# Q and K of a banded attention kernel cut into full 128-row tiles, with the static order retuned

A kernel for sliding-window attention followed by a mixture of adapters was already tuned. One change regroups the rows of queries and keys so that every transpose works on a full tile, retunes the order in which the engines' work is emitted, adds matmuls at the start that only keep TensorE busy, and moves the fetching of the adapter weights.

## The chip, the cores and the metric

The kernel runs on one core of one Trainium2 chip. The metric is device time in microseconds of one execution. Each run is marked fast or slow (slow: over 1.5% above the fastest run of the same kernel), and comparisons use fast runs. A ratio below is the mean time of one kernel's fast runs over that of the other's of the same rounds, so it is not quite the ratio of the medians that I quote. Its 95% interval is in brackets. A profile shows one execution, and its span is about 1.7 us shorter than the time of that run.

Engines in the profile: PE is TensorE (matmuls), PEld its weight loads, DVE is VectorE, ACT ScalarE, POOL GpSimd, SP SyncE, whose queue (SPq) issues nearly all transfers (36.58 of 38.27 MB in before).

## The reference

Eight batches of eight heads, 576 positions, 64 channels. Attention sees a band of 32 positions to each side. The 512 attention outputs of a position are then the input of a two-of-eight mixture of rank-16 adapters.

```python
scores = (q @ k.transpose(0, 1, 3, 2)) / np.sqrt(64)       # [8, 8, 576, 576]
scores = np.where(np.abs(pos[:, None] - pos[None, :]) <= 32, scores, -1e9)
attn = softmax(scores)
x = (attn @ v).transpose(0, 2, 1, 3).reshape(8 * 576, 512)
logits = x @ w_gate                                         # [4608, 8]
# the two largest logits of a row, softmax over the two: weights w
delta = sum over the two chosen e of  w[e] * (x @ A[e]) @ B[e]   # ranks 16
out = x + delta
```

q, k, v are normal with deviation 0.1, so the scores are tiny and the softmax inside the band is nearly flat.

## The kernel before

A batch is worked on as four units; a unit is a pair of heads (n and n + 4), whose 64 channels each fill 128 partitions once transposed. The steps, with the names that the profile uses:

1. load q, k, v from memory as float32 into `r` tiles (SyncE's queue, in order);
2. POOL casts them to float16: `c` for q and k, `vbd` for v;
3. PE transposes q and k into the PSUM tile `tp`; DVE and ACT copy it to `qT` and `kT`;
4. PE forms score tiles `ps` (first the mask, then q against k), ACT takes the exponential into `PT`;
5. PE multiplies with v into `po`, DVE normalizes into `xb`;
6. adapters: PE transposes (`tx`), multiplies with gate and A (`pz`), DVE computes the gate and the gated product `zs`, PE transposes it (`tz`) and multiplies with B (`pd`), ACT copies out (`obt`), SyncE's queue stores.

With 576 positions split into pairs of neighbours, one head has 288 rows of 128 values: two full tiles of 128 rows and a stub of 32.

```python
    def load_qk(b, w, eng, n0=0, n1=NP):
        ...
        src = (q, k)[w][b].rearrange("(e n) (p j) d -> e p n (j d)", e=2, j=2)
        for g in range(3):                       # two full row groups and the stub
            r0, r1 = 128 * g, min(128 * g + 128, S // 2)
            if g < 2:
                dst = raw[b, w][:, g]
            else:
                dst = raw[b, 3][32 * w:32 * w + 32]
            ...
    def transposes(u, which, holder):            # one unit, q or k
        ...
        for g in range(3):
            p0, np_ = (0, 128) if g < 2 else (32 * which, 32)
            for j in range(2):
                ...
                nc.tensor.matmul(
                    out=o, lhsT=src[:, g, j, n] if g < 2 else sx[p0:p0 + 32, j, n],
                    rhs=ident[p0:p0 + np_, p0:p0 + np_], is_transpose=True,
                    start=True, stop=True)
```

So a unit takes four full transposes and two stubs for q and as many for k: eight groups of six a batch, 48 in all, 16 of them stubs.

The weights of the adapters are fetched on POOL's queue right at the start, in pieces that transfer and convert at once (0.27 MB in 4832 packets):

```python
    def load_weights():
        for c in range(4):
            nc.gpsimd.dma_start(out=WA_sb[:, c, 0:ER],
                in_=moe_A.transpose([1, 0, 2])[128 * c:128 * c + 128])
        nc.gpsimd.dma_start(out=WA_sb[:, :, ER:],
            in_=moe_w_gate.rearrange("(c p) e -> p c e", p=128))
        nc.gpsimd.dma_start(out=B_sb, in_=moe_B.rearrange("e r d -> (e r) d"))
```

The order of the instructions on each engine is static. A small scheduler inside the program lists all operations with estimated durations and a due time each, simulates, and emits them in the order found. The due times come from one table, in units of a quarter batch (`DUE`: `ld` loads, `cqk` casts of q and k, `cv` cast of v, `tq` and `tk` transposes, `g0` and `g3` the gate, and so on). When an operation has to wait, what stands behind it on the engine waits too: in g, below, six casts of q and k stand behind a V cast with which POOL waits 6.0 us, and start right after the V casts.

The softmax here doesn't subtract the row's maximum and nothing guards it: scores larger than these inputs give would overflow.

## Time and profile before

| | before |
|---|---|
| median, 3 runs | 175.34 us (174.99 to 175.36) |
| span of the profiled execution | 172.3 us |
| PE busy | 137.2 us |
| first transpose starts | 11.4 us |
| pace, gate of batch 1 to gate of batch 6, by batch | 16.9 us |

From the page of before: part 1 (busy time, share of span, instructions) and three rows of part 2, in which each character is one fortieth of the span, 4.3 us, and a digit is tenths of busy time (PE), of granted TensorE clock (PEclk) or of the 16 DMA engines' time (DMA).

```profile
PE 137.2 (80%) x1600; PEld 103.4 (60%) x1600; DVE 113.8 (66%) x290; ACT 85.0 (49%) x109; POOL 85.0 (49%) x91
...
PE   0028596699957999999599989997999899969180
...
PEclk9999999659995699999999999999999999999968
DMA  5999999999999899999999997976889603403425
```

Three stretches show. PE is idle at first, uneven until slice 14 (60 us) with two dips of the clock (0.50 at 32 to 38 us, 0.52 at 52 to 58), then nearly full until slice 35 (150 us). DMA is full from the second slice to the 24th. Both PE and DMA are candidates for the limit in the middle.

The idle start, in the table of waits of before (waiting engine and line, what ended the wait: total us, times, longest) and in the timeline of POOL (start, duration, engine, line, operation):

```profile
PE tp L360 <- POOL c L197: 11.6, 2, 11.4
```

```profile
5.73 3.74 POOL L263 DMA_DIRECT2D WA_sb<-in_moe_A_dram  x4
...
10.74 1.20 POOL L197 CAST c<-r 128x512 f16<-128x512 f32 x2
```

The first transpose waited 11.4 us for a cast on POOL, which was issuing weight transfers until 10.7.

The transposes in the groups of before, different shapes apart (line, engine, operation, output and input, shape, count, busy us and mean ns of one, idle time before them and what ended it):

```profile
L360 PE MATMUL tp<-ident,c 128*128 128x128 f16 x256 | 28.0, 238 | 21.4 <-POOL c L197 11.6 <-DVE qT L366 8.1 <-ACT kT L376 1.6
L360 PE MATMUL tp<-ident,c 32*128 32x32 f16 x128 | 13.7, 181 | 2.4 <-POOL c L204 2.4
...
L360 PEld LDWEIGHTS <-c 128*128 128x128 f16 x256 | 19.1, 104 | 23.9 <-POOL c L197 12.8 <-issue 9.2
L360 PEld LDWEIGHTS <-c 32*128 32x128 f16 x128 | 7.2, 95 | 10.6 <-POOL c L204 3.1 <-issue 2.4
```

The records of the stubs, 181 ns, are little shorter than those of full tiles, 238 ns. The records overlap: a group's four and two come to 1.3 us at these means, and below the group takes 0.46. The timeline of PE in before, in the full stretch:

```profile
85.31 0.61 PE L409 MATMUL ps<-qT,kT 128*128 128x128 f16 x8
85.76 0.53 PE L360 MATMUL tp<-ident,c 128*128 128x128 f16 x6
86.22 0.60 PE L404 MATMUL ps<-mask,ident 128*128 128x512 f16 x2
```

A group of six (four full and two stubs) starts at 85.76 and the next work at 86.22: 0.46 us.

### The profile page before, as it was taken

How to read it: one execution, taken by the hardware profiler on the slowest of the kernel's cores; microseconds unless marked ns; L12 is line 12 of the kernel's file. 1: busy time of each engine (PE TensorE's matmuls, PEld its weight loads, DVE VectorE, ACT ScalarE, POOL GpSimd, SP SyncE). 2: the span in 40 equal slices, each digit the busy share in tenths (PEclk: the TensorE clock that was granted, in tenths of full speed). 3: DMA queues.
4: the chain of work that ended last, by engine and by line, in shares of the span. 5: the costliest groups of instructions: out<-in, count | busy, mean ns of one | idle time of the engine just before them, and what ended most of it. 6: DMA issues, size and time to landing. Idle time of an engine off the chain costs nothing.

```text
span 172.3 us, 4079 instructions
## 1 busy us (share of the span) xinstructions
PE 137.2 (80%) x1600; PEld 103.4 (60%) x1600; DVE 113.8 (66%) x290; ACT 85.0 (49%) x109; POOL 85.0 (49%) x91
## 2 busy tenths in 40 slices
PE   0028596699957999999599989997999899969180
PEld 0015365468945776878486868785867677857020
DVE  6877527428799278957785787678848967784600
ACT  0021453156423656575379466744693577365150
POOL 7994955785785684474558335934291400000000
PEclk9999999659995699999999999999999999999968
DMA  5999999999999899999999997976889603403425
GB/s 147 206 196 235 233 341 226 232 310 257 208 325 280 186 294 295 200 296 305 277 217 276 344 294 179 317 218 194 195 297 227 248 4 107 167 4 121 153 74 200
DMA packets 85809, 38.27 MB, mean 222 GB/s; under 512 B 44192, under 2 KB 81184, under 8 KB 85792
## 3 DMA queue, kind: packets, MB, share of 16 engines
q1 hardware_dynamic: 78464, 36.58, 80.4%
q0 software_dynamic: 4832, 0.27, 4.6%
q10 hardware_dynamic: 2496, 1.18, 2.5%
q8 instruction: 12, 0.20, 0.5%
q14 instruction: 5, 0.04, 0.1%
HBM read 28.85 MB, written 9.44 MB: 222 GB/s over the span
## 4 chain that ended last, share of the span: by engine, by line
PE 63%; DMA 13%; DVE 11%; ACT 4%; SPq 2%; issue 2%; ACTq 2%; POOL 1%
PE po L445 13%; PE tp L360 10%; DMA r<-in_k_dram 10%; PE ps L404 8%; PE ps L409 7%; PE pz L497 6%; PE pd L554 6%; PE tx L481 5%; PE pd L556 5%; DMA r<-in_q_dram 3%; DVE dm L519 2%; SPq L175 2%; ACT PT L416 2%; PE tz L541 2%; DVE qT L366 2%
## 5 line engine op out<-in xcount | busy, mean ns | idle before, releaser
L360 PE MATMUL tp<-ident,c 128*128 128x128 f16 (+1 forms) x384 | 37.0, 219 | 23.8 <-POOL c L197 11.6
L360 PEld LDWEIGHTS <-c 128*128 128x128 f16 (+1 forms) x384 | 26.3, 101 | 34.5 <-POOL c L197 12.8
L197 POOL CAST c<-r 128x1024 f16<-128x1024 f32 (+1 forms) x36 | 32.3, 906 | 28.2 <-DMA r<-in_k_dram 15.3
L416 ACT ACTIVATE PT<-ps 128x1024 f16<-128x1024 f32 x36 | 36.8, 1024 | 16.9 <-PE ps L409 16.2
L211 POOL CAST vbd<-r 64x2304 f16<-64x2304 f32 (+1 forms) x20 | 35.0, 1748 | 20.2 <-DMA r<-in_v_dram 10.0
L376 ACT COPY kT<-tp 64x576 f16<-64x576 f16 x32 | 20.3, 634 | 32.1 <-DVE kT L374 31.7
L445 PE MATMUL po<-vbd,PT 128*128 128x130 f16 x416 | 28.7, 220 | 1.1 <-ACT PT L416 0.7
L409 PEld LDWEIGHTS <-kT 128*128 128x128 f16 x288 | 21.7, 107 | 10.6 <-issue 3.6
L459 DVE TENSOR_TENSOR xb<-po,rc 128x640 f16<-128x640 f32 x32 | 26.4, 825 | 1.1
L445 PEld LDWEIGHTS <-PT 128*128 128x128 f16 x416 | 24.8, 97 | 2.7 <-ACT PT L416 0.9
L409 PE MATMUL ps<-qT,kT 128*128 128x128 f16 x288 | 24.7, 235 | 0.0
L404 PE MATMUL ps<-mask,ident 128*128 128x512 f16 x72 | 24.5, 426 | 0.0
L561 ACT COPY obt<-pd 128x1024 f32<-128x1024 f32 (+1 forms) x24 | 20.4, 871 | 7.9 <-PE pd L556 7.7
L488 DVE COPY xT<-tx 128x512 f16<-128x512 f16 x40 | 15.5, 419 | 11.3 <-PE tx L481 11.0
L374 DVE COPY kT<-tp 64x576 f16<-64x576 f16 x32 | 14.2, 445 | 9.1 <-PE tp L360 9.1
L366 DVE COPY qT<-tp 128x576 f16<-128x576 f16 x32 | 14.5, 452 | 5.3 <-PE tp L360 5.1
L554 PE MATMUL pd<-B_sb,zT 128*128 128x512 f16 x40 | 16.0, 400 | 1.6 <-ACT zT L546 1.6
L556 PE MATMUL pd<-xb,perm 128*128 128x512 f16 x40 | 15.9, 399 | 0.0
L458 DVE RECIPROCAL rc<-po 128x10 f32<-128x10 f32 x32 | 6.9, 216 | 12.8 <-PE po L445 12.8
L481 PE MATMUL tx<-ident,xb 128*128 128x128 f16 x160 | 13.3, 221 | 0.0
L481 PEld LDWEIGHTS <-xb 128*128 128x128 f16 x160 | 10.5, 99 | 2.5
L497 PE MATMUL pz<-WA_sb,xT 128*128 128x136 f16 x160 | 10.8, 223 | 0.0
(44 smaller groups left out, 99.1 us busy)
## 6 DMA issues: line engine op xcount, KB each, us to landing
r<-in_v_dram SPq DMA_DIRECT2D x24, 288.0 KB, 6.0
r<-in_q_dram SPq DMA_DIRECT2D x12, 512.0 KB, 5.7
r<-in_k_dram SPq DMA_DIRECT2D x12, 512.0 KB, 6.6
out_dram<-obt SPq DMA_DIRECT2D x24, 256.0 KB, 3.0
out_dram<-obt SPq DMA_DIRECT2D x16, 192.0 KB, 3.1
r<-in_q_dram SPq DMA_DIRECT2D x22, 128.0 KB, 4.5
r<-in_v_dram SPq DMA_DIRECT2D x16, 144.0 KB, 3.7
r<-in_k_dram SPq DMA_DIRECT2D x14, 128.0 KB, 3.0
```

The lines of the kernel that those rows point to most:

```text
L197: eng.tensor_copy(out=qk[b, w][:, g, :, n0:n1].rearrange("p j n e d -> p e n j d"), in_=raw[b, w][:, g, :, n0:n1].rearrange("p e n (j d) - ...
L211: eng.tensor_copy(out=dst[64 * e:64 * e + 64, NB * n0:NB * n1, VD * e:VD * e + D], in_=raw[b, 2][64 * e:64 * e + 64, NB * n0:NB * n1])
L360: nc.tensor.matmul(out=o, lhsT=src[:, g, j, n] if g < 2 else sx[p0:p0 + 32, j, n], rhs=ident[p0:p0 + np_, p0:p0 + np_], is_transpose=True, ...
L404: nc.tensor.matmul(out=ps[:, i:i + 4], lhsT=ident, rhs=mask.rearrange("p r h j k -> p (r h j k)"), start=True, stop=False)
L409: nc.tensor.matmul(out=ps[:, i], lhsT=kTs[u % NQ][:, a, :], rhs=qTs[u % NQ][:, :, 32 * a:32 * a + 64].rearrange("p j (h k) -> p h j k", h= ...
L416: nc.scalar.activation(out=PTs[t % NPT][:, :, 64:192], in_=holder["t"], func=AF.Exp, scale=1.0 / float(D) ** 0.5)
L445: nc.tensor.matmul(out=po[:, GS * g:GS * g + 2 * VD], lhsT=PTs[t % NPT][:, sl, off:off + 128], rhs=vbd[b % NV][:, n, a, :], start=(i == 0) ...
L459: nc.vector.tensor_tensor(out=xs[b].rearrange("p g (e n d) -> p g e n d", e=2, n=NP)[:, :, :, n], in0=pog[:, :, :, 0:D], in1=bcast(rc, 3, ...
L481: nc.tensor.matmul(out=tp[:, 128 * c:128 * c + 128], lhsT=xs[b][:, g, 128 * c:128 * c + 128], rhs=ident, is_transpose=True, start=True, st ...
L497: nc.tensor.matmul(out=pz[:, GS * g:GS * g + ER + E], lhsT=xT[:, g, c, :], rhs=WA_sb[:, c, :], start=(c == 0), stop=(c == 3))
L554: nc.tensor.matmul(out=pd[:, i], lhsT=zT[:, g], rhs=B_sb, start=True, stop=False)
L556: nc.tensor.matmul(out=pd[:, i], lhsT=perm, rhs=xs[b][:, g], start=False, stop=True)
```

## The change

Four heads of 288 row pairs are 1152 rows, which is nine tiles of 128 exactly. The change strings the four heads together before cutting, so that stubs are gone: 36 full transposes a batch in six groups, one `c` tile in three equal chunks, two transfers of 128 partitions for q or k of one batch instead of three (v keeps its four transfers of 32 partitions). Head borders now fall inside a tile, so a query copy out of PSUM is in two pieces, and the scores wait for chunks instead of units. Also: the table of due times is new; 20 dummy matmuls run before the first transposes; the first batch is loaded by thirds; the weights are fetched in batch 1.

```diff
-DUE = dict(ld=-10.42, cqk=-6.15, cv=-3.48, tq=-3.24, tk=-2.87, s=-0.73, e=-19.89,
-           pv=-0.4, nm=1.98, tx=-0.8, txs=0.14, pz=0.7, g0=3.1, g3=1.41, tz=2.88,
-           pd=3.21, pds=0.86, st=-7.0)
+DUE = dict(ld=-4.69, cqk=-23.42, cv=-8.79, tq=-3.2, tk=-2.65, s=-0.62, e=-6.89,
+           pv=0.47, nm=0.13, tx=-0.2, txs=-2.15, pz=0.3, g0=-18.05, g3=-5.45,
+           tz=2.29, pd=3.33, pds=3.07, st=-1.9)
...
+        src = (q, k)[w][b].rearrange("(e n) s d -> e (n s) d", e=2)
+        src = src.rearrange("e (i p j) d -> e p i (j d)", p=128, j=2)
+        for e in range(2):
+            eng.dma_start(out=raw[b, w][:, e, 3 * c0:3 * c1], in_=src[e][:, 3 * c0:3 * c1])
...
+    def warm():
+        wt = pw.tile([128, 1024], F32, tag="w", name="warm")
+        for i in range(NWARM):                      # NWARM = 20
+            nc.tensor.matmul(out=wt[:, 0:512], lhsT=ones[:, 0:128], rhs=ones,
+                             start=True, stop=True)
...
-    c_w = P.op("POOL", 5.0, 21, load_weights, [c_perm])
...
-    def transposes(u, which, holder):
+    def transposes(b, c, w, holder):                # chunk c of 3, w: q or k
...
-        for g in range(3):
-            p0, np_ = (0, 128) if g < 2 else (32 * which, 32)
+        for i in range(3):
             for j in range(2):
...
+                nc.tensor.matmul(out=o, lhsT=src[:, 3 * c + i, j], rhs=ident,
+                                 is_transpose=True, start=True, stop=True)
...
+        if b == 1:
+            P_w.append(P.op("POOL", 5.5, 2, load_weights, [P_cast[0, 2, 3], c_perm]))
```

Cut: the matching edits of casts, copies and dependences.

## The prediction

> **What bounds it now** (table of stretches, timeline).
>
> - 0 to 11.4 us: TensorE does nothing; its first transpose waits 11.4 us for a POOL cast (table of waits). The weight-load issues hold POOL from 5.7 to 10.7 us.
> - 11 to 60 us: data arrives late. Batch 1's keys land at 28.8 us (chain of waits). TensorE finishes batch 0's attention at 28.4, then starves, and much runs at half clock: granted clock about 0.5 at 32-38 and 52-58 us; the score mask pair takes 0.96 us there, 0.43 later.[...]
> - 60 to 148 us: TensorE is about 95% busy, some 17.4 us a batch. The chain is matmuls: per batch 8 transpose groups x 0.45, 4.5 score tiles x 0.88, 4 PV x 0.78, tx 1.1, pz 1.2, tz 0.4, pd 2.15: about 15.7 us. DMA is a close second: its share is about 1.0 until 112 us. Loads alone repeat every 13.4 us (queue issues), stores add about 3.4: 16.7 us a batch. V's issues hold the queue 5.8 us against 3.7 for as many bytes of q; V moves in 256 B rows.[...]
>
> **What changes.**
> - Transposes: 48 a batch (16 of them 32-row stubs costing nearly as much as full ones) become 36. At 0.075 us each: -0.9 us of TensorE a batch; about 4.5 us of it lies in the TensorE-bound stretch.
> - Copies out of PSUM: DVE keys 4x0.445 -> 3x0.57, ACT 4x0.634 -> 3x0.82, queries 4 -> 6 smaller ones (1.8 -> about 1.95 us a batch). No net gain.
> - POOL: q/k casts 5.2 -> 4.8 us a batch; V casts, now halves, 4.2 -> 4.65. Equal.
> - DMA: same bytes and rows; two full-width issues per tensor instead of three. DMA time hardly falls, so it caps the steady state near 16.7 us.
> - Start: thirds instead of halves, POOL free at 5.5 us: first transpose at about 7 instead of 11.4. The weights' DMA work is moved, not removed; in batch 1 it competes with loads and holds POOL 5 us. Worth 2-3 us.
> - Twenty dummy matmuls[...] occupy TensorE from 1.5 to about 9 us[...], but nothing fills the gaps at 29 and 48 us; at most 1-2 us.
> - The retuned order runs the gate early on DVE and may fill early gaps: 2 us, the least certain term.
>
> **Sum.** 4.5 + 2.5 + 1 + 2 = about 10 us of 175.3. The tail (last pz at 158 us, then gate chain, pd and stores, 14 us) stays.
>
> **Predicted: 165.5 us, 80% range 158 to 172.** Faster by over 2%: 0.86; within 2%: 0.10; slower: 0.04.
>
> **Right if:** transpose matmuls 384 -> 288, their busy time 37 -> about 28 us; period (pz to pz) 17.4 -> 16.5-16.8; first real transpose by 8 us; DMA share near 1.0 to about 110 us; tail near 14 us. **Wrong if:** period below 16 (the stubs or the old order cost more, or DMA got more efficient without 32-partition transfers), or still 17.4 (DMA is the real limit).
>
> **What would spoil it:** transposes now wait for the scores of the batch two earlier, so buffers free in coarser steps; two-piece DVE copies hold the two transpose PSUM buffers longer; weights in batch 1 delay its casts and batch 0's pz; dummies delay the first transposes; the new order could bunch stores at the end.

The 1 us for the dummies stands as my estimate alone. Estimates, too, are the figures after the arrows; the control measured 0.54 us for a copy of keys on DVE and 0.79 on ACT, 1.8 us a batch for the copies of queries, and 4.7 and 4.6 us a batch for POOL's casts of q and k and of V.

## More of the kernel before

Last, the pace. The first operation of the gate runs once a batch, right after `pz`; in the timeline of DVE in before:

```profile
47.58 0.20 DVE L514 TENSOR_REDUCE m<-pz 128x5 f32<-128x40 f32 x1 [0.64 <-PE pz L497]
65.09 0.20 DVE L514 TENSOR_REDUCE m<-pz 128x5 f32<-128x40 f32 x1 [0.84 <-PE pz L497]
...
149.53 0.20 DVE L514 TENSOR_REDUCE m<-pz 128x5 f32<-128x40 f32 x1 [0.22 <-PE pz L497]
159.50 0.20 DVE L514 TENSOR_REDUCE m<-pz 128x5 f32<-128x40 f32 x1 [0.76 <-PE pz L497]
```

These are batches 0, 1, 6 and 7. From batch 1 to 6 it is (149.53 - 65.09) / 5 = 16.9 us a batch. I use these marks to tell where time went: start (to batch 1), middle (to batch 7), tail (12.8 us, to the end of the span).

## The result, and the profile after

| | before | after |
|---|---|---|
| median | 175.35 us (4 runs, 174.99 to 176.65) | 168.53 us (4 runs, 167.57 to 170.10) |
| ratio of fast runs | | 0.958 [0.951, 0.965] |
| second set of rounds, medians | 174.58 us | 166.89 us |
| ratio of these | | 0.961 [0.955, 0.967] |

The change is faster by about 4%. The forecast gain was 9.8 us and 6.8 us came. The profiled run of the first set fell into the slow state (170.1 us), so I read the profile of after from the second set, whose profiled run was fast (167.57 us, span 165.8); it is the same kernel.

The same views of after. The page:

```profile
PE 132.2 (80%) x1524; PEld 101.4 (61%) x1524; DVE 111.1 (67%) x290; ACT 83.0 (50%) x101; POOL 83.6 (50%) x104
...
PE   6927977279187998899799949998999899695380
...
PEclk9996999969855899999999996999999999999567
DMA  4999999999999899999998999999996033108016
```

PE now starts at once (the dummies), has holes at about 8, 29 and 41 us (digits 2, 2 and 1), and then is nearly full. PE's busy time fell by 5.0 us although it now contains 7.2 us of dummies. DMA is full until about slice 30 (124 us).

The transposes as one group, and in PE's timeline of after:

```profile
L357 PE MATMUL tp<-ident,c 128*128 128x128 f16 x288 | 24.0, 225 | 13.1 <-POOL c L185 8.5
```

```profile
85.67 0.50 PE L357 MATMUL tp<-ident,c 128*128 128x128 f16 x6
86.00 0.38 PE L565 MATMUL pd<-B_sb,zT 128*128 128x512 f16 x1
```

Six full transposes now take 0.33 us from start to next start, 0.055 us each (granted clock 1.00), against 0.46 us for the four and two before. At a granted clock of 0.50, at 46.30 us in after, six took 0.61 us. A batch has six groups instead of eight: 8 x 0.46 = 3.7 us became 6 x 0.33 = 2.0 us.

POOL no longer holds up the first cast (timeline of POOL in after):

```profile
5.70 0.83 POOL L185 CAST c<-r 128x768 f16<-128x768 f32 x1
...
19.28 1.78 POOL L253 DMA_DIRECT2D WA_sb<-in_moe_A_dram  x2
```

The gate, once a batch (timeline of DVE in after; batches 0, 1, 6 and 7):

```profile
41.45 0.20 DVE L525 TENSOR_REDUCE m<-pz 128x5 f32<-128x40 f32 x1 [0.15 <-PE pz L508]
62.51 0.20 DVE L525 TENSOR_REDUCE m<-pz 128x5 f32<-128x40 f32 x1
...
141.38 0.20 DVE L525 TENSOR_REDUCE m<-pz 128x5 f32<-128x40 f32 x1
152.22 0.20 DVE L525 TENSOR_REDUCE m<-pz 128x5 f32<-128x40 f32 x1 [1.45 <-PE pz L508]
```

Between these two profiles the span fell by 6.5 us:

| part | before | after | difference |
|---|---|---|---|
| to the gate of batch 1 | 65.1 | 62.5 | -2.6 |
| batch 1 to batch 7 | 94.4 | 89.7 | -4.7 |
| tail | 12.8 | 13.6 | +0.8 |

The pace from batch 1 to 6 is (141.38 - 62.51) / 5 = 15.8 us.

One line in the table hides a loss. At batch 0, after is 6.1 us ahead (41.45 against 47.58); at batch 1 only 2.6 us are left. The windows of after around that place give, by stretch, its length, then the busy us of PE, PEld, DVE, ACT and POOL, each with its number of instructions, then the granted clock, the DMA share and GB/s (the same columns in every windows view below):

```profile
20.00:24.00 4.00, 2.72 (x40) 2.03 (x38) 2.60 (x7) 2.73 (x3) 3.78 (x6) 1.00 2.20 208
24.00:28.00 4.00, 3.04 (x44) 2.50 (x42) 2.97 (x8) 1.37 (x2) 3.32 (x5) 1.00 1.92 140
...
40.00:44.00 4.00, 1.92 (x30) 1.51 (x26) 3.26 (x11) 0.31 (x2) 1.99 (x3) 1.00 0.97 286
44.00:48.00 4.00, 1.70 (x17) 1.71 (x18) 2.77 (x7) 0.00 (x0) 3.01 (x5) 0.57 1.11 334
```

From 20 to 28 us, while the weights come, the transfers' times add up to twice the engines' time and yet move only 208 and 140 GB/s. From 40 to 48 PE is busy for 3.6 of 8 us, waiting for casts of batch 2, whose data is late. The queue that issues loads (timeline of SyncE in after) shows why they are late:

```profile
17.52 16.27 SPq L179 DMA_DIRECT2D r<-in_v_dram  x8
33.90 2.37 SPq L170 DMA_DIRECT2D r<-in_q_dram  x2
```

V of batches 1 and 2 hold the queue from 17.5 to 33.8 us; q of batch 2 comes after them.

### The profile page after: what moved, and what is told of

It reads as the page before. It is cut to its first block, busy times and chain, and to the rows that moved or that the text cites. A ratio compares the mean times of both kernels' runs of the same rounds, so it can differ in the third digit from the quotient of the medians.

```text
span 168.3 us, 3876 instructions
## 1 busy us (share of the span) xinstructions
PE 130.1 (77%) x1524; PEld 100.3 (60%) x1524; DVE 112.4 (67%) x290; ACT 83.1 (49%) x101; POOL 83.4 (50%) x104
## 4 chain that ended last, share of the span: by engine, by line
PE 47%; DVE 18%; DMA 15%; SPq 10%; POOL 3%; issue 2%; ACT 2%; ACTq 0%; POOLq 0%
DMA r<-in_k_dram 15%; PE po L456 11%; PE pd L565 6%; PE pd L567 6%; SPq L170 6%; PE tp L357 5%; PE tx L492 5%; PE ps L415 5%; PE ps L420 4%; SPq L179 4%; DVE zs L542 3%; PE pz L508 3%; POOL c L185 3%; PE tz L552 2%; DVE xb L470 1%
## 5 line engine op out<-in xcount | busy, mean ns | idle before, releaser
L185 POOL CAST c<-r 128x768 f16<-128x768 f32 x47 | 37.3, 825 | 26.0 <-DMA r<-in_q_dram 10.6
L193 POOL CAST vbd<-r 64x1152 f16<-64x1152 f32 x32 | 37.1, 1158 | 19.2 <-DMA r<-in_v_dram 17.5
L427 ACT ACTIVATE PT<-ps 128x1024 f16<-128x1024 f32 x36 | 36.3, 1024 | 17.6 <-PE ps L420 17.4
L357 PE MATMUL tp<-ident,c 128*128 128x128 f16 x288 | 24.9, 230 | 20.3 <-POOL c L185 14.6
L456 PE MATMUL po<-vbd,PT 128*128 128x130 f16 x416 | 30.7, 226 | 5.2 <-ACT PT L427 2.1
L377 ACT COPY kT<-tp 64x768 f16<-64x768 f16 x24 | 19.0, 793 | 29.8 <-DVE kT L375 29.6
L357 PEld LDWEIGHTS <-c 128*128 128x128 f16 x288 | 19.4, 103 | 23.1 <-POOL c L185 16.3
L456 PEld LDWEIGHTS <-PT 128*128 128x128 f16 x416 | 26.6, 101 | 6.3 <-issue 3.2
L420 PEld LDWEIGHTS <-kT 128*128 128x128 f16 x288 | 20.8, 104 | 10.9 <-issue 2.9
L470 DVE TENSOR_TENSOR xb<-po,rc 128x640 f16<-128x640 f32 x32 | 26.4, 825 | 1.1
L499 DVE COPY xT<-tx 128x512 f16<-128x512 f16 x40 | 15.7, 420 | 12.7 <-PE tx L492 12.3
L375 DVE COPY kT<-tp 64x768 f16<-64x768 f16 x24 | 13.0, 544 | 9.1 <-PE tp L357 8.9
L366 DVE COPY qT<-tp 128x576 f16<-128x576 f16 (+2 forms) x48 | 14.7, 347 | 6.2 <-PE tp L357 6.2
```

The source lines that it names most:

```text
L185: eng.tensor_copy(out=qk[b, w][:, 3 * c:3 * c + 3].rearrange("p i j e d -> p e i j d"), in_=raw[b, w][:, :, 3 * c:3 * c + 3].rearrange("p ...
L193: eng.tensor_copy(out=dst[64 * e:64 * e + 64, NB * n0:NB * n1, VD * e:VD * e + D], in_=raw[b, 2][64 * e:64 * e + 64, NB * n0:NB * n1])
L357: nc.tensor.matmul(out=o, lhsT=src[:, 3 * c + i, j], rhs=ident, is_transpose=True, start=True, stop=True)
L420: nc.tensor.matmul(out=ps[:, i], lhsT=kTs[u // NP % 2][:, u % NP * NB + a, :], rhs=qTs[u // NP % 2][:, :, u % NP, 32 * a:32 * a + 64].rear ...
L427: nc.scalar.activation(out=PTs[t % NPT][:, :, 64:192], in_=holder["t"], func=AF.Exp, scale=1.0 / float(D) ** 0.5)
L456: nc.tensor.matmul(out=po[:, GS * g:GS * g + 2 * VD], lhsT=PTs[t % NPT][:, sl, off:off + 128], rhs=vbd[b % NV][:, n, a, :], start=(i == 0) ...
```

## The experiments

The theory that I started from is the prediction's: TensorE has less to do per batch, and the start is earlier. The rivals: (R1) the gain is the new order, not the regrouping; (R2) the missing part was lost in the start, to the weights' transfers or to V's place in the queue; (R3) the dummies matter. The quoted expectations name the theories in their own way. All kernels give correct results unless I say otherwise.

| run | what it is | median us | ratio to before [95%] |
|---|---|---|---|
| x_after_again | after, unchanged | 166.89 | 0.961 [0.955, 0.967] |
| a_weights_early | after, weights at the start | 167.44 | 0.961 [0.954, 0.968] |
| b_v_after_k | after, V queued later | 169.65 | 0.970 [0.963, 0.978] |
| e_no_weights | after, weights not fetched | 162.94 | 0.933 [0.927, 0.940] |
| d_no_warm | after, no dummies | 168.10 | 0.964 [0.956, 0.971] |
| g_old_due | after, old due times | 176.42 | 1.003 [0.994, 1.011] |
| i_structure | regrouping alone | 175.64 | 1.009 [1.002, 1.015] |
| h_full_stubs | before, stubs made full | 172.24 | 0.981 [0.973, 0.989] |
| j_before_new_due | before, new due times | 200.39 | 1.135 [1.127, 1.143] |
| k_casts_due | after, old due times but for the casts | 175.56 | 0.999 [0.992, 1.005] |
| f_packed_weights | after, weights in plain rows | 179.98 | 1.020 [1.012, 1.027] |
| f2_packed_aligned | the same, tiles aligned | 166.23 | 0.954 [0.950, 0.959] |

The first three rows and the fourth ran on one chip in the same rounds; d, g, i, h on a second; j, k, f on a third; f2 on a fourth. Each ratio is to before on its own chip, whose medians were 174.58, 175.24, 174.27 and 173.39 us.

### x_after_again: the change once more

No edit.

> Control: the changed kernel as it is, on the chip of the next three runs. About 0.96 of before, 167.5 to 169 us. Its profile should again show the hole of TensorE at 40 to 48 us, with batch 2's keys landing near 47 us.

It measured 166.89 us, ratio 0.961 [0.955, 0.967]: the first result stands. It is 0.6 us below the times I had expected; the hole is there (the windows above). It is the control for what follows.

### a_weights_early: the weights back at the start

```diff
-    c_perm = P.op("POOL", 0.4, -98, init_perm, [c_ident])
+    c_perm = P.op("POOL", 0.4, -98, lambda: (init_perm(), load_weights()), [c_ident])
...
-            P_w.append(P.op("POOL", 5.5, 2, load_weights, [P_cast[0, 2, 3], c_perm]))
+            P_w.append(P.op("POOL", 5.5, 2, lambda: None, [P_cast[0, 2, 3], c_perm]))
```

The planned order of everything else is the same, so only the place of the fetch differs.

> The changed kernel with the weight loads back at the start, right after the constants; every other instruction keeps its order. Theory 1 (the weights' small transfers in batch 1 slow the loads of batches 1 and 2 and make the hole at 40 to 48 us): batch 2's keys land 3 to 5 us earlier, but the first casts start 5 us later; total 1 to 3 us less. Theory 2 (batch 2's V queued ahead of its q and k makes the hole): the keys land within 2 us of the control, total the same or 1 to 2 us more for the late first cast. Theory 3 (the hole does not matter, what follows absorbs it): within 1 us.

It measured 167.44 us, ratio 0.961 [0.954, 0.968], against 0.961 for the control of the same rounds: no difference, which Theories 2 and 3 both allow. The windows of this run show the same slow stretch, only earlier:

```profile
8.00:16.00 8.00, 2.15 (x24) 1.70 (x24) 6.17 (x12) 0.79 (x1) 7.88 (x10) 0.79 1.93 182
```

182 GB/s at a share of 1.93, and PE busy for 2.15 of 8 us. The queue reached q of batch 2 at 32.98 us, against 33.90 in the control. POOL was held at the start again, and the first transpose came at 11.6 us instead of 8.5; that cost nothing either. Moving the weights is worth nothing measurable: their cost is moved, as the prediction had said.

### e_no_weights: no weights at all

```diff
-            P_w.append(P.op("POOL", 5.5, 2, load_weights, [P_cast[0, 2, 3], c_perm]))
+            P_w.append(P.op("POOL", 5.5, 2, lambda: (nc.gpsimd.memset(WA_sb, 0.01),
+                nc.gpsimd.memset(B_sb, 0.01)), [P_cast[0, 2, 3], c_perm]))
```

The result is wrong (relative error 0.28); this gives the price of the fetch, the 5 us of POOL that issue it included.

> Wrong result on purpose: the weights are not loaded but set to a constant by two POOL memsets at the same place. Theory 1: GB/s at 20 to 32 us rises from about 175 to about 300, batch 2's keys land 5 us earlier, total falls by 4 to 6 us. Theory 2: bandwidth rises but the order still holds the keys back, total falls by 1 to 2 us. Theory 3: total within 1 us.

It measured 162.94 us, ratio 0.933 [0.927, 0.940]: 4 us under the control of the same rounds. The fetch moves 0.27 MB of 38 MB and costs 2.4% of the time. Windows of this run:

```profile
20.00:24.00 4.00, 3.10 (x46) 2.55 (x45) 2.59 (x7) 2.73 (x3) 0.82 (x1) 1.00 1.05 279
```

With no weights the stretch moves 279 GB/s at a share of 1.05 (control: 208 at 2.20), from 24 to 28 us 184 at 0.82 (control: 140 at 1.92), and batch 1's gate comes at 57.8 instead of 62.5 us. (This profile is of a slow run, 166.26 us; the ratio is of fast ones.) So part of R2 holds: the weights cost time at the start. But they did so in before as well (its window from 8 to 16 us: 198 GB/s at a share of 1.75), so this is no reason for a smaller gain.

### b_v_after_k: V of a batch queued behind its q and k

```diff
         assert len(order) == n, (len(order), n)
+        for b in range(8):
+            vs = [o for o in order if o.get("tag") == (b, 2)]
+            k = max(i for i, o in enumerate(order) if o.get("tag") == (b, 1))
+            if len(vs) == 1 and order.index(vs[0]) < k:
+                order.insert(k, order.pop(order.index(vs[0])))
```

This moves V of batch 2 behind q and k of batch 2, and nothing else in practice.

> The changed kernel with one swap in the DMA queue: batch 2's V is issued after its q and k, not before. Theory 1 (weights): keys of batch 2 still late, total within 1 us of the control. Theory 2 (order of the queue): keys land 5 to 7 us earlier, the hole shrinks to under 3 us and the total falls by 3 to 5 us. Theory 3 (absorbed later): the hole shrinks, but the total moves by less than 1 us.

It measured 169.65 us, ratio 0.970 [0.963, 0.978]: about 1% slower than the control of the same rounds, though the intervals overlap; in any case not faster. The early part did what it should. In its timelines, q of batch 2 is issued at 27.57 us (control 33.90), and the gate of batch 1 comes at 57.62 us, 4.9 us earlier. But batch 6's gate comes at 141.93 us, against 141.38. All of the lead is given back. The queue of SyncE in this run shows a place where that happens:

```profile
73.23 1.70 SPq L175 DMA_DIRECT2D r<-in_q_dram  x2
75.03 3.63 SPq L585 DMA_DIRECT2D out_dram<-obt  x1
78.76 1.73 SPq L175 DMA_DIRECT2D r<-in_k_dram  x2
```

A store stands in the queue between q and k and holds it for 3.63 us (a single store at 108.56 us: 0.43), most likely waiting for its data, and the load of k behind it goes out only at 78.76. This is a shift by one part of an order that was made for another timing. That these stores ate all of the lead I have not isolated. What is shown is that an earlier batch 1 alone does not end the program earlier: the hole of the start is real, but filling it was not worth its 5 us.

### d_no_warm: no dummy matmuls

```diff
-    NWARM = 20
+    NWARM = 0
```

> The changed kernel without the twenty dummy matmuls; nothing else differs. If the dummies help[...]: the first transposes at 7 to 15 us run at half rate, and the total grows by 1 to 2 us over the control's 0.96 of before. If they are idle decoration ([...]data is what is waited for): within 0.7 us, ratio 0.957 to 0.965.

It measured 168.10 us, ratio 0.964 [0.956, 0.971], against 0.961 [0.955, 0.967] for the control on another chip: no effect to be seen, and not more than about 1% in any case. PE's timelines say why. This one is of the run without dummies,

```profile
6.58 0.82 PE L357 MATMUL tp<-ident,c 128*128 128x128 f16 x6 [6.58 <-POOL c L185]
...
13.10 1.72 PE L357 MATMUL tp<-ident,c 128*128 128x128 f16 x12 [4.71 <-POOL c L185]
14.62 1.06 PE L415 MATMUL ps<-mask,ident 128*128 128x512 f16 x2
```

and this one of the control:

```profile
1.46 7.23 PE L240 MATMUL warm<-ones 128*128 128x512 f16 x20 [1.46 <-DVE ones L286]
8.53 0.83 PE L357 MATMUL tp<-ident,c 128*128 128x128 f16 x12
12.84 0.49 PE L357 MATMUL tp<-ident,c 128*128 128x128 f16 x6 [3.48 <-POOL c L185]
...
14.62 1.06 PE L415 MATMUL ps<-mask,ident 128*128 128x512 f16 x2
```

With dummies the first 12 transposes do run fast, in 0.83 us; without, two groups of six take 0.82 us each. The granted clock reads 1.00 from 0 to 12 us in both runs; that the dummies raise the clock is not shown. But the transposes start 2 us later, both kernels then wait for the next cast, and both start the first score tile at 14.62 us, in 1.06 us for two mask matmuls that take 0.59 later. R3 falls.

### g_old_due: the new structure with the old due times

```diff
-DUE = dict(ld=-4.69, cqk=-23.42, cv=-8.79, tq=-3.2, tk=-2.65, s=-0.62, e=-6.89,
-           pv=0.47, nm=0.13, tx=-0.2, txs=-2.15, pz=0.3, g0=-18.05, g3=-5.45,
-           tz=2.29, pd=3.33, pds=3.07, st=-1.9)
+DUE = dict(ld=-10.42, cqk=-6.15, cv=-3.48, tq=-3.24, tk=-2.87, s=-0.73, e=-19.89,
+           pv=-0.4, nm=1.98, tx=-0.8, txs=0.14, pz=0.7, g0=3.1, g3=1.41, tz=2.88,
+           pd=3.21, pds=0.86, st=-7.0)
```

> The changed kernel's structure with the priorities of the kernel before. If the retuned order is a main part of the gain: 2 to 5 us slower than the control (ratio 0.97 to 0.99). If the gain is the structure's (full tiles): within 1 us, ratio about 0.96.

It measured 176.42 us, ratio 1.003 [0.994, 1.011]. The whole gain is gone, more than either expectation allowed, with the regrouping, the dummies and the moved weights all in place. Batch 0's gate still comes early (39.55 us); the loss is in the pace, (151.88 - 65.45) / 5 = 17.3 us a batch. (This profile is of a slow run, 177.85 us; the fast one of i, below, gives (148.09 - 62.63) / 5 = 17.1.) In its table of waits:

```profile
POOL vbd L193 <- PE po L456: 19.6, 4, 6.0
```

POOL waits 19.6 us in four places with a V cast that may not overwrite the V of two batches earlier until PE has used it. In the control's table the V casts wait for PE for 0.7 us in all. The casts of q and k stand behind it on POOL and are late: after the longest of these waits, 6.0 us, two V casts run from 96.99 us and the six of q and k from 99.41.

### i_structure: the regrouping alone

Old due times as in g, weights at the start as in a, and NWARM = 0. The first batch's loads by thirds remain.

> Full tiles alone: old priorities, no dummies, weight loads at the start, as in the kernel before. If the saved TensorE time (6 transposes in 0.33 us against 0.47 us for 4 full and 2 stubs) is nearly the whole gain: ratio 0.955 to 0.97. If order, dummies and weights carry it: 0.98 to 1.0.

It measured 175.64 us, ratio 1.009 [1.002, 1.015]: the regrouping by itself, in the order that suited the kernel before, is worth nothing, or a little less. The wait of POOL for PE is there too, 18.6 us, here in a fast run.

### h_full_stubs: what the stubs cost

The kernel before, with each stub replaced by a transpose of a full tile (of other data) into the place where it belongs:

```diff
+                if g == 2:
+                    b0 = 256 + 288 * j if which == 0 else 512 + 128 * j
+                    o = tp[:, b0:b0 + 128]
+                    nc.tensor.matmul(out=o, lhsT=src[:, 1, j, n], rhs=ident,
+                                     is_transpose=True, start=True, stop=True)
+                    continue
```

This does not compute the reference: the last rows of each head hold others' data. It passed the comparison, most likely because the scores are so small that the softmax hardly depends on them. So it is a probe, not a kernel to use. It does more arithmetic than before. It also drops a wait of PE for the stubs' cast; in the table of before that wait was 2.4 us in total, all of it before batch 1's gate.

> Wrong result on purpose: the kernel before with each 32-row stub transpose replaced by a full 128x128 transpose of other data; still 48 a batch. Theory A (the stubs themselves are slow, more than a full transpose[...]): a group of six falls from about 0.47 to 0.33 us[...], about 1 us a batch, total 2 to 6 us less than before (ratio 0.965 to 0.99). Theory B (each transpose costs about 0.078 us whatever its rows, only the count matters): a group of six stays at 0.47 us, total within 1 us of before.

It measured 172.24 us, ratio 0.981 [0.973, 0.989]. Replacing small transposes by larger ones made the program 2% faster, as Theory A expected. PE's timeline in this run:

```profile
85.89 0.39 PE L366 MATMUL tp<-ident,c 128*128 128x128 f16 x4
86.11 0.28 PE L363 MATMUL tp<-ident,c 128*128 128x128 f16 x2
86.22 0.28 PE L450 MATMUL po<-vbd,PT 128*128 128x130 f16 x2
```

Four full ones take 0.22 us, and the two that replace stubs take 0.11. In before the six took 0.46, so the pair of stubs added about 0.46 - 0.22 = 0.24 us: 0.12 for each, on average twice a full tile. The records' own durations (181 against 238 ns) had suggested the opposite. Nor do the weight loads by themselves (95 against 104 ns in before) explain the 0.24 us.

The single records of before do. Here are the stubs of the group at 85.76 in the timelines of PE and of its weight loads:

```profile
86.08 0.21 PE L360 MATMUL tp<-ident,c 32*128 32x32 f16 x2
86.08 0.11 PEld L360 LDWEIGHTS <-c 32*128 32x128 f16 x2
```

The last full transpose of the group starts at 85.93, the first stub only at 86.08. In the 42 groups of before from 60 to 150 us, the medians from one start to the next are 55 ns from full to full, 151 ns from full to stub, 39 ns from stub to stub, and 104 ns from a stub to the score or value matmul that follows most groups. The weight load of a full tile starts 2 ns after the start of the matmul before it; that of a stub behind a full tile starts 147 ns after, and that of the work behind a stub 99 ns after. So it is not the stub that is slow: two stubs in a row are closer than two full tiles. The change of shape is, twice a group, because there the weight load no longer runs ahead. What in the change holds the load back (the fewer rows, or something else in which the two differ) no run separates.

Over 64 groups 0.13 us each is 8.3 us of TensorE's work; 2% of 175 us, about 3.4 us, came out. The pace went from 16.9 to (145.44 - 63.17) / 5 = 16.5 us. From the gate of batch 1 to that of batch 6, where the dropped wait plays no part, the gain is 84.44 - 82.27 = 2.2 us, for 40 groups and 5.0 us of TensorE's work.

### j_before_new_due: the old structure with the new due times

The edit of g in reverse, on the kernel before.

> The kernel before with nothing but the new priorities. If the order is good in itself: 2 to 4 us less than before (ratio 0.975 to 0.99). If each set of priorities only fits the structure it was tuned for: no gain or a loss (ratio 1.0 to 1.04), since the old set gave the new structure no gain either (1.003).

It measured 200.39 us, ratio 1.135 [1.127, 1.143]. The new order on the old structure is a disaster of 13%, far beyond what I had expected. The same wait, on the other side:

```profile
POOL vbd L211 <- PE po L445: 40.1, 4, 11.5
```

With g, i and j, R1 falls as well as the plain form of my theory. Structure and order are not two terms of a sum. Regrouping alone +0.9%, new order alone +13.5%, both -4%. Each order was tuned for one structure and breaks on the other, with POOL held by V casts as the most visible sign.

### k_casts_due: is it the due times of the casts?

The kernel of g with only the two due times of the casts new:

```diff
-DUE = dict(ld=-10.42, cqk=-6.15, cv=-3.48, ...
+DUE = dict(ld=-10.42, cqk=-23.42, cv=-8.79, ...
```

> The new structure with the old priorities, except the two of the casts (q/k casts and V casts), which are the new ones. Theory C (under the old set V casts stand in POOL's queue ahead of the next batch's q/k casts and wait for PV, 19.6 us of such waits at 60 to 150 us, so transposes come late): most of the loss comes back, ratio 0.96 to 0.98, and that wait falls below 6 us. Rival D (the gain lies in the order on DVE and TensorE, gate, norm and transposes): the wait falls but the ratio stays at 0.99 to 1.01.

It measured 175.56 us, ratio 0.999 [0.992, 1.005], and the wait stayed (both this profile and g's are of slow runs):

```profile
POOL vbd L191 <- PE po L454: 18.1, 4, 8.4
```

The edit did not remove what it was meant to remove (19.6 us became 18.1), so it does not tell whether removing that wait would bring the gain. It does tell that the casts' due times alone do not carry it. Which of the 18 due times do stays open.

### f_packed_weights: cheaper weights

Since the weights cost 4 us, I tried to fetch them with plain copies of whole rows (256 B, 128 B and 2 KB) on SyncE's queue, and to convert on POOL. The contraction index is permuted so that the rows are contiguous; `pz` reads its other operand with a stride of 4.

```diff
+    A_raw = const.tile([128, E, 4 * R], F32)
+    G_raw = const.tile([128, 4 * E], F32)
+    B_raw = const.tile([128, DD], F32)
+
+    def fetch_weights():
+        nc.sync.dma_start(out=A_raw, in_=moe_A.rearrange("e (p c) r -> p e (c r)", c=4))
+        nc.sync.dma_start(out=G_raw, in_=moe_w_gate.rearrange("(p c) e -> p (c e)", c=4))
+        nc.sync.dma_start(out=B_raw, in_=moe_B.rearrange("e r d -> (e r) d"))
...
-                             lhsT=xs[b][:, g, 128 * c:128 * c + 128],
+                             lhsT=xs[b].rearrange("p g (k c) -> p g c k", c=4)[:, g, c],
```

> A candidate better than both: the changed kernel with the weights fetched by three plain transfers in rows of 256 bytes, 128 bytes and 2 KB (about 1,300 rows in place of 4,700) on the sync queue before batch 1's q, and cast on POOL; the contraction index is permuted to match (every fourth column of x goes into one transpose). Without any weight load the kernel took 4 us less than the control. If that cost lies in the many short rows: 2.5 to 4 us of it comes back, ratio 0.935 to 0.95, and the slow stretch at 20 to 28 us (174 GB/s) disappears. If it lies in the bytes or in POOL's time alone: under 1 us, ratio about 0.96.

It measured 179.98 us, ratio 1.020 [1.012, 1.027], 6% above the control and outside both expectations. Only 2 of its 6 runs counted as fast. The time was not lost at the weights but everywhere. Windows of this run, in the middle of the program where no weights move:

```profile
60.00:80.00 20.00, 16.59 (x194) 13.30 (x193) 15.38 (x36) 11.37 (x15) 12.56 (x14) 0.91 1.15 228
```

228 GB/s, where the control moves 302. Addresses in this program are static, and the three new tiles (2048, 128 and 2048 B a partition) lie in front of the load tiles. In before and after, all tiles for the loads of q, k and v and for the stores start at a multiple of 512 B within a partition (so say the addresses in the built programs). Here they start 128 B past one.

### f2_packed_aligned: the same with one pad

```diff
-    G_raw = const.tile([128, 4 * E], F32)
+    G_raw = const.tile([128, 128], F32)          # 512 B instead of 128 B a partition
```

and the copy and the cast use its first 32 columns.

> The kernel after with the weights fetched by three plain copies on the sync queue (rows of 256 B, 128 B and 2 KB) and converted on POOL, as in f_packed_weights, but one constant is padded so that all large tiles start 512-byte aligned within a partition again, as they do in every other kernel of this study (in f_packed_weights they stood 128 bytes off). Theory A (the offset slowed every transfer): DMA between 60 and 80 us is back at about 300 GB/s (f: 228), V's four issues hold the queue 6.3-7.0 us again (f: 7.7-8.1), and the ratio to the kernel before is 0.935 to 0.95, about 163 to 166 us, since the run without weights was 4 us under the kernel after. Rival B (the plain weight copies themselves, or the weight columns read with a stride of 4 by the loads of pz, are what was slow): DMA stays near 230 GB/s and the ratio at 1.0 or above. Rival C (offset was it, but the packed rows save nothing over the cut-up ones): 300 GB/s and about 0.96.

It measured 166.23 us, ratio 0.954 [0.950, 0.959]. Windows of this run:

```profile
60.00:80.00 20.00, 18.52 (x255) 15.37 (x253) 16.13 (x45) 11.79 (x15) 13.75 (x15) 1.00 1.12 305
```

The rate is back at 305 GB/s, and 6.5 points of ratio hung on 384 bytes of padding. In the DMA records of the two traces, the 37,888 packets of 256 B took 26.4 ns on average when misaligned and 20.2 ns when aligned; the 36,864 of 512 B took 32.1 and 28.2 ns. That is +31% and +14%. The 2 KB packets, nearly all stores out of tiles that were as far off, show no such effect: 94.1 ns misaligned, 94.8 aligned. By what mechanism the offset costs a load this much, no run shows. (The misaligned trace is of a slow run, the aligned one of a fast run; the ratios come from fast runs of both.)

So the theory of the offset is settled, and the hope of f is too: with the offset mended, plain rows gain no more than 0.6% on the control, with intervals that overlap ([0.950, 0.959] and [0.955, 0.967], on different chips). f2 beats before by 4.6% and has the lowest ratio of the correct kernels, but that it beats after is not shown. Nor is it shown, then, that the many small pieces are what the weights cost: in f2 the stretch from 20 to 28 us moves 327 and 247 GB/s, and batch 1's gate still comes at 62.0 us (control 62.5, e 57.8).

## Why the prediction was right or wrong, point by point

The time fell within the range, 3 us above the forecast. The sum was 4.5 + 2.5 + 1 + 2 = 10 us.

- **"At 0.075 us each: -0.9 us of TensorE a batch"** was mis-sized. I spread 0.45 us over six transposes alike. In fact a full one takes 0.055 us, and a pair of stubs with the two changes of shape around it 0.24 us (h), so 3.7 us became 2.0, -1.7 us a batch. I had written that stubs cost "nearly as much as full ones"; between full tiles they cost twice as much. For the same reason the busy time of the transposes fell from 37.0 to 24.0 us, not to 28.
- **"Period 17.4 to 16.5-16.8"**: by the eight gates it was 16.9 and became 15.8. The base was read too high and the decrease too small. This is, just, the "wrong if" branch of a period below 16 (15.9 in a, 16.0 in d, 15.7 in f2; 16.2 in the slow first profile of after), and h shows the first of the causes I listed there (stubs cost more), g and i the second (the order).
- **"DMA time hardly falls, so it caps the steady state near 16.7 us"**: the first half held. The times of all DMA packets add up to 152.0 us of the 16 engines in before and 151.8 us in the control. The cap failed: the batches now come at 15.8 us. DMA does not look like what set the pace, in either kernel: the last batch counted, from the gate of batch 5 to that of batch 6, took 17.9 us in before at a DMA share of 0.44 and 15.9 us in after at 0.29, no less than the average. And a share near 1 did not mean that no more could be moved. In the windows from 60 to 120 us, the three kernels with the old load shape (before, h, j) move 265 to 267 GB/s at very different speeds, and the ten aligned profiles with the new shape move 280 to 288, those of slower kernels (g 281, i 288) too: 7% more in the control (286 against 266). The third branch ("DMA got more efficient without 32-partition transfers") is not shown by this: the 32-partition transfers of v are still there, and in that window a packet of 512 B took 28.4 ns in before and 28.1 in the control (256 B: 20.5 and 19.9; 2 KB: 99.8 and 93.3). The larger part of the 7% is the share, from 1.00 to 1.05; why it rose, no run isolates.
- **"4.5 us in the TensorE-bound stretch"**: the middle gave 4.7 us. The number is right by luck, for two wrong reasons that cancel: less work by twice as much, and only part of it on the critical path (h: 2.2 us of 5.0). And it is not the regrouping's own gain: alone, the regrouping gives nothing (i).
- **"The retuned order ... 2 us, the least certain term"** is the step that failed most. The order is not a term to be added. Without it the other parts gain nothing (g: 1.003); without them it costs 13.5% (j).
- **"Start: worth 2-3 us"**: 2.6 us at batch 1. The first real transpose came at 7.3 us in the first profile of after and at 8.5 in the control, against "by 8 us"; a, with 11.6, shows that it hardly matters. I did not foresee that 6 us of lead at batch 0 would shrink to 2.6 at batch 1; b shows that keeping the lead would not have helped in this order.
- **"The weights' DMA work is moved, not removed"** was right (a: no difference; e: the fetch costs 4 us wherever it stands).
- **Dummies "at most 1-2 us"**: nothing that could be told from noise (d). The 1 us in the sum was not there.
- **"The tail ... stays"**: 12.8 us became 13.6, against the 14 I had named.

In short: of the forecast 10 us, 7 came in start and middle as predicted by place (2.6 + 4.7), the 3 us for order and dummies did not come on top, and the tail took 0.8 back.

## What to carry to other kernels

Where the records of matmuls overlap, cost one from the start of one to the start of the next, for each pair of shapes apart: here two small leftover tiles between full ones took more time than four full ones (0.24 against 0.22 us) while their records look shorter (181 against 238 ns), and the time went at the changes of shape (151 and 104 ns from start to start, against 55 from full to full). In a kernel with a static order, a new structure and its retuned order are one change; test neither alone to judge the other, and do not add them up in a forecast (here 1.009 and 1.135 alone, 0.96 together). When an edit adds a constant tile and everything gets slower, look at the addresses of the tiles behind it before looking at the edit (here 384 bytes of padding: 1.020 against 0.954, 228 against 305 GB/s).
